# Attention keys and own queries turned on VectorE in 32x32 tiles, with softmax sums taken by columns of ones

## The chip, the cores and the metric

The kernel runs on one core of one Trainium2 chip. The metric is the device time of one execution in microseconds (us): 1069.41 us before the change, the median of three runs (1069.33 to 1069.71). The profile names the engines PE (TensorE; PEld is its loading of weights), DVE (VectorE), ACT (ScalarE), POOL (GpSimd) and SP (SyncE, whose queue issues nearly all DMAs).

## The reference

There are 8 batches of 576 tokens, and 8 heads of 64 columns. Per head, queries are normalised over the head's 64 columns and keys over the 576 tokens; the output is queries x (keys transposed x values). Then comes a Fourier mixing layer with a two-layer network:

```python
q_s = softmax(q, axis=-1)            # exp(q - max) / (sum + 1e-9)
k_s = softmax(k, axis=2)             # over the 576 tokens
kv  = einsum('bhsd,bhse->bhde', k_s, v)
x   = einsum('bhsd,bhde->bhse', q_s, kv)   # put together as (batch, token, 512)
u   = x + real(fft(fft(x, axis=1), axis=2))
un  = (u - mean(u)) / sqrt(var(u) + 1e-6)
out = u + relu(un @ w_ch1) @ w_ch2   # 512 -> 2048 -> 512
```

All is fp32.

## The kernel before, in words

The network of one batch takes most of TensorE's time. Batch 0 goes through it plainly (`plain`, the plain stage), while the weights are converted and combined. From then on `up` and `down` (`deep_down`) use Strassen's seven products; one pass of both is called an order, and order n works on one group of tokens while attention, mixing and normalisation of batch n + 1 are prepared beside it. Every step is a small function with a planned time; `timed` lists them for each order, all are sorted by that time, scaled by 0.87, and written out in that order. So the planned times fix the order of the instructions of every engine, and each engine works its list in order.

In the product stage (`up`), four rounds of seven products run. Each product of a round collects in one of three PSUM banks, ba, bb and bc. The order of products is 1, 6, 5, 7, 2, 4, 3: product 1 in ba is copied to s1 by ACT; after product 6 DVE adds u2 = bb + s1 (L1216), and only then may product 7 collect further in bb; after product 7 DVE adds u3 in the same way, and only then comes product 4. POOL combines the results of a round in a chain of four steps (`a_side`, L383 to L386). The weights come through a ring of four chunks (`load`, `used`, L454).

Attention of batches 2 to 7 is laid out by `attention_timed`. It starts with the product stage in orders 1 and 2 (`start` is 0), and 7 planned units ahead of it later. Two heads form a region of 128 columns, so there are four regions of keys. Keys come transposed in DRAM as (column, token). Per region:

- `k_exp`: maximum over the tokens on DVE (L666), exponential with the sum in one pass on ACT (L672), inverse on DVE;
- `k_turn`: four transposes on TensorE into a PSUM tile (L690), copied by ACT (L696), and a fifth for the last 64 tokens (L700), copied by DVE (L704);
- `k_times_v`: five products with the values (L716) into a bank named acc, of which there are three; DVE scales them into `kvr` (L724).

There are four tiles of own queries (128 tokens each) in every batch. Per tile:

- `q_exp`: maximum per head on DVE (L760), eight exponentials with a bias each on ACT (L766), sums, inverse and, for two of the four tiles, normalisation on DVE (L785 to L796);
- `q_turn`: four transposes on TensorE (L824), copied by ACT, reversed for two tiles (L834);
- `q_times_kv`: four products with `kvr` (L886), taken out by DVE with the inverse (L901) or copied by ACT (L903).

A ninth tile of shared tokens (`t_...`) is made once for two batches. Batches 0 and 1 have steps of their own (`first_keys`, `opening`, and the plain stage); they share some of these functions.

In fp32 a product appears in the trace as two MATMUL passes, a transpose as one.

## Time and profile before

| | us |
|---|---|
| median of three runs | 1069.41 (1069.33 to 1069.71) |
| span of the profiled execution | 1068.4 |
| time around the span, by the median | 1.0 |
| busy: PE, PEld | 1056.4, 920.5 |
| busy: DVE, ACT, POOL | 698.9, 398.2, 380.4 |
| product passes of `up` (L1246): 1792 | 431 (184.2 + 123.8 + 123.4) |
| product stages of orders 1 to 4 begin at | 177.7, 296.9, 413.5, 528.7 |

The busy time of an engine is the time in which at least one of its instructions ran; TensorE's overlap, so that the length of one MATMUL is more than the distance to the next. Idle time of an engine that is not the bottleneck costs nothing. The page holds one execution, and its span leaves out what lies before the first and behind the last instruction. The granted clock of TensorE was 1.000 over the span.

### The profile page before, as it was taken

The numbers are of one execution on the slowest core, as the hardware profiler recorded it, in microseconds if no ns is written. First come the engines' busy times: TensorE is split into PE (matmuls) and PEld (weight loads), VectorE is DVE, ScalarE is ACT, GpSimd is POOL, SyncE is SP. The second block draws the span as 40 slices with busy tenths as digits, with TensorE's granted clock in tenths as the row PEclk, the third lists the DMA queues.
The fourth block names the chain that finished last, engine by engine and source line by source line (L and its number), as shares of the span: only waits on it lengthen the run. The fifth ranks groups of instructions, "written<-read, shape, count | busy, mean of one in ns | idle before, by whom it ended". The sixth has DMA issues, their size and how long they took to land.

```text
span 1068.4 us, 16964 instructions
## 1 busy us (share of the span) xinstructions
PE 1056.4 (99%) x6394; PEld 920.5 (86%) x6394; DVE 698.9 (65%) x1350; ACT 398.2 (37%) x925; POOL 380.4 (36%) x321
## 2 busy tenths in 40 slices
PE   8999999999999999999999999999999999999998
PEld 7744556988898899889998999889988998899898
DVE  6898887675455785677555765678457654674563
ACT  5674433642245215631443234521552132231210
POOL 3263320265511734454515542384336350000000
PEclk9999999999999999999999999999999999999999
DMA  8687578648976576646755576557644575576464
GB/s 266 237 294 251 179 244 294 205 156 284 331 257 207 195 254 235 226 165 209 262 192 193 197 242 213 198 200 257 223 168 158 198 253 181 194 260 221 173 215 151
DMA packets 113546, 236.04 MB, mean 221 GB/s; under 512 B 23272, under 2 KB 74856, under 8 KB 102840
## 3 DMA queue, kind: packets, MB, share of 16 engines
q1 hardware_dynamic: 113096, 234.42, 64.3%
q8 instruction: 51, 0.84, 0.3%
q10 hardware_dynamic: 288, 0.26, 0.1%
q14 instruction: 31, 0.25, 0.1%
q0 software_dynamic: 80, 0.26, 0.1%
HBM read 199.79 MB, written 39.06 MB: 224 GB/s over the span
## 4 chain that ended last, share of the span: by engine, by line
PE 88%; DVE 1%; ACT 1%; issue 0%; POOL 0%; ACTq 0%
PE bb L1246 16%; PE bc L1246 10%; PE ba L1246 10%; PE bb L1373 10%; PE bc L1373 7%; PE ba L1373 7%; PE bb L1343 5%; PE acc L716 3%; PE acc L886 2%; PE bc L1183 2%; PE bb L1462 2%; PE acc L999 2%; PE acc L1002 2%; PE acc L1027 2%; PE bc L1462 1%; PE ba L1462 1%
## 5 line engine op out<-in xcount | busy, mean ns | idle before, releaser
L1246 PE MATMUL bb<-unT,big 128*128 128x256 f32 x768 | 184.2, 379 | 0.0
L1246 PEld LDWEIGHTS bb<-unT,big 128*128 128x128 f32 x768 | 142.7, 190 | 18.7 <-DVE u L1216 0.6
L1258 ACT ACTIVATE big<-big 128x512 f32<-128x512 f32 x96 | 60.4, 629 | 195.7 <-DVE big L1257 195.3
L1246 PE MATMUL ba<-unT,big 128*128 128x256 f32 x512 | 123.8, 379 | 0.0
L1246 PE MATMUL bc<-unT,big 128*128 128x256 f32 x512 | 123.4, 379 | 0.0
L1216 DVE TENSOR_TENSOR u<-bb,s 128x512 f32<-128x512 f32 x66 | 45.5, 689 | 104.8 <-PE bb L1246 84.6
L383 POOL TENSOR_TENSOR big<-big 128x512 f32<-128x512 f32 x24 | 30.5, 1269 | 224.6 <-ACT big L1258 224.6
L1246 PEld LDWEIGHTS bc<-unT,big 128*128 128x128 f32 x512 | 94.7, 190 | 12.4 <-DVE big L1257 0.8
L1373 PE MATMUL bb<-big 128*128 128x128 f32 x848 | 105.1, 275 | 0.3 <-DVE u L1380 0.3
L1246 PEld LDWEIGHTS ba<-unT,big 128*128 128x128 f32 x512 | 94.4, 190 | 12.2 <-issue 0.5
L1373 PEld LDWEIGHTS bb<-big 128*128 128x128 f32 x848 | 99.6, 192 | 0.5 <-DVE u L1380 0.4
L1323 POOL TENSOR_TENSOR x<-x,big 128x512 f32<-128x512 f32 x45 | 57.7, 1296 | 62.1 <-issue 32.3
L1373 PE MATMUL ba<-big 128*128 128x128 f32 x640 | 79.6, 275 | 0.0
L1373 PEld LDWEIGHTS ba<-big 128*128 128x128 f32 x640 | 76.3, 192 | 1.2
L1319 DVE TENSOR_TENSOR big<-big 128x512 f32<-128x512 f32 x98 | 75.3, 806 | 0.0
L766 ACT ACTIVATE q<-q,qm 128x64 f32<-128x64 f32 x216 | 58.5, 338 | 25.4 <-DVE qm L760 18.9
L1380 DVE TENSOR_TENSOR u<-bb,s 128x256 f32<-128x256 f32 x40 | 16.8, 421 | 65.0 <-PE bb L1373 61.6
L1343 PE MATMUL bb<-big 128*128 128x256 f32 x256 | 58.7, 381 | 0.0
L1257 DVE TENSOR_TENSOR big<-bc,u 128x512 f32<-128x512 f32 x64 | 43.9, 686 | 21.8 <-PE bc L1246 21.0
L1122 POOL TENSOR_TENSOR unT<-unT 128x512 f32<-128x512 f32 x8 | 14.2, 1771 | 123.4 <-DVE unT L1122 100.8
L1343 PEld LDWEIGHTS bb<-big 128*128 128x128 f32 x256 | 48.2, 190 | 8.0 <-DVE big L1257 1.1
L1373 PE MATMUL bc<-big 128*128 128x128 f32 x416 | 51.5, 275 | 0.0
(268 smaller groups left out, 2028.4 us busy)
## 6 DMA issues: line engine op xcount, KB each, us to landing
big<-w2d SPq DMA_DIRECT2D x67, 1024.0 KB, 4.8
big<-w1s SPq DMA_DIRECT2D x64, 896.0 KB, 4.8
big<-w2s SPq DMA_DIRECT2D x16, 1024.0 KB, 6.6
big<-in_w_dram SPq DMA_DIRECT2D x21, 512.0 KB, 6.2
w2d<-big SPq DMA_DIRECT2D x42, 256.0 KB, 5.4
q<-in_q_dram SPq DMA_DIRECT2D x28, 256.0 KB, 6.6
k<-in_kT_dram SPq DMA_DIRECT2D x24, 288.0 KB, 5.5
v<-in_v_dram SPq DMA_DIRECT2D x24, 256.0 KB, 4.5
```

The costliest lines, as they stand in the source:

```text
L383: e1.tensor_tensor(out=to(4), in0=at(2), in1=at(3), op=ALU.add)
L716: nc.tensor.matmul(pk, lhsT=ks[:, c, :], rhs=v[:, c, :], start=(c == 0), stop=(c == NC - 1))
L766: nc.scalar.activation(q[:, h, :], q[:, h, :], ACT.Exp, bias=m[:, h:h + 1])
L1216: plus = lambda t: V.tensor_tensor(out=temp(t), in0=box["bb"][:], in1=box["s1"][:], op=ALU.add)
L1246: nc.tensor.matmul(bank()[:, i, :], lhsT=w[:, WA_AT[m], k * P:(k + 1) * P], rhs=self.unT[g][:, B_AT[m], k, :], start=first and i == 0 and ...
L1257: steps = [(0, lambda: V.tensor_tensor(out=hp(i), in0=bank()[:], in1=u()[:], op=ALU.add)), (0.8, lambda: nc.scalar.activation(hp(i), hp(i) ...
L1258: (0.8, lambda: nc.scalar.activation(hp(i), hp(i), ACT.Relu))]
L1319: e.tensor_tensor(out=to(o), in0=to(x), in1=to(y), op=op)
L1323: E.tensor_tensor(out=x, in0=x, in1=tile(m), op=ALU.add)
L1343: nc.tensor.matmul(box[name][:, i, :], lhsT=h[p][:, A_AT[m], i * P:(i + 1) * P], rhs=self.stream[n][:, p, :], start=p == 0 and (m != 1 or ...
L1373: nc.tensor.matmul(box[place[n]][:, i, :], lhsT=own(m)(A_AT[n])[:, f, :], rhs=w[:, r // 2, r % 2 * P:r % 2 * P + P], start=first and f == ...
L1462: nc.tensor.matmul(bank()[:, i, :], lhsT=h[p][:, A_AT[m], i * P:(i + 1) * P], rhs=w[:, p, :], start=first and i == 0 and p == 0, stop=p == ...
```

## The change

- Keys of a batch are loaded into one tile `kb` of 128 partitions: token block i (160 tokens, the last overlapping) lies on partitions 32 i to 32 i + 31, and 16 groups of 32 columns lie behind one another. Four loads on 32 partitions each replace four on 128. Values go into `vt` in the same manner, in two halves of 256 columns, four loads per half, with a column of ones at each end.
- `keys`: one maximum per region on DVE over 4 x 160 elements, joined over the four partition groups by ACT copies and DVE minima; 16 exponentials on ACT without a sum; DVE turns a region in 32x32 tiles, region 0 into a free buffer and each further one into the place of the region before it; five products with 129 columns, of which one is ones and gives the sums of the exponentials.
- `own_exp`: maximum on DVE, subtraction on POOL, turning on DVE in 32x32 tiles, then 16 exponentials on ACT that put the 32x32 tiles in their place on the way (reversed for two tiles). `own_times_kv`: products with 130 columns, two of them ones, and the inverse of the sums on DVE; the output is written in two halves by DVE, and uses two acc banks.
- The planned times of these steps and of the loads are new, `prepare` sets the ones on POOL in the plain stage, and the last four blocks of the second layer's weights are combined in another order.

Batches 0 and 1 and the shared tiles keep their transposes on TensorE. The core of the diff:

```diff
-            t = c.tile([P, NR, P], F32, name=f"kvr{b}")
+            t = c.tile([P, NR, P + 2], F32, name=f"kvr{b}")
...
-        self.kss = [c.tile([P, NC, P], F32, name=f"ks{i}") for i in range(2)]
...
-        self.kss += [self.work.tile([P, NC, P], F32, tag="v", name="ks", bufs=2) for _ in range(2)]
-        for t in self.kss[:2]:
-            nc.gpsimd.memset(t[0:64, 4, :], 0.0)
+        self.kb = c.tile([P, NR, 4, NC * Q], F32, name="kb")
+        kb = self.kb[:].rearrange("p r g s -> p (r g s)")
+        self.kss = [kb[:, i * NC * P:(i + 1) * NC * P].rearrange("p (c n) -> p c n", n=P) for i in range(NR)]
+        self.vt = c.tile([P, NC, 2 * P + 2], F32, name="vt")
...
-        keys = [("k", b, r) for r in range(NR)]
         tail = [("t", b)] if b % 2 == 0 else []
         own = [("q", b, c, u) for c, u in ((0, 0), (0, 1), (1, 1), (1, 0))]
-        first = start + 14 + 5 * len(tail)
-        gap, steps = (end - 13.7 - first) / 3, []
-        places = [first + gap * i for i in range(4)]
-        shared = start + 14
-        if tail and start == 0:
-            shared, places = 17, [14, 21, 26, 31.3]
-        for i, it in enumerate(keys):
-            t = start + 3.5 * i
-            if i > 1:
-                steps += at(t - 5, self.k_load(it)[:1]) + at(t + 1.8, self.k_load(it)[1:])
-            steps += at(t, self.k_exp(it)) + at(t + 4, self.k_turn(it)) + at(t + 7, self.k_times_v(it))
+        places, shared = [6, 13.5, 21.5, 27.2], start + 12
+        if tail:
+            places = [8.5, 14, 21.5, 27.2]
+        if start == 0:
+            places, shared = [13.5, 20.5, 24, 27.2], 7
+        steps = at(start, self.keys(b))
         for it in tail:
             steps += at(shared, self.q_exp(it)) + at(shared + 8, self.t_turn(it))
             steps += at(22.4 if start < 0 else 35, self.t_fold(it))
         for t, it in zip(places, own):
-            steps += at(t, self.q_exp(it)) + at(t + 8.7, self.q_turn(it)) + at(t + 12.1, self.q_times_kv(it))
-        loads = [(t, self.q_load(it)) for t, it in zip(places, own)] + [(shared - 6, self.t_load(it)) for it in tail]
+            steps += at(t, self.own_exp(it)) + at(t + 15, self.own_times_kv(it))
+        loads = [(t - 7, t + 7.6, self.own_load(it)) for t, it in zip(places, own)]
+        loads += [(shared - 13, shared + 8.4, self.t_load(it)) for it in tail]
         loads.sort(key=lambda s: s[0])
-        for t, load in loads[2:]:
-            steps += at(t - 6, load)
-        return steps + at((33 if start < 0 else 39) if tail else 22, self.t_times_kv(b))
+        free = [-99] * 3
+        for i, (t, end, load) in enumerate(loads):
+            if i > 1:
+                steps += at(max(t, free[-3]), load)
+            free.append(end)
+        return steps + at((33 if start < 0 else 39) if tail else max(22, start + 26), self.t_times_kv(b))
...
-        steps = [(20 + r, lambda r=r: self.keys_to(b, r)) for r in range(3)]
-        steps += [(35 + r, lambda r=r: self.values_to(b, r)) for r in range(2)]
-        q = [self.q_load(("q", b, 0, u)) for u in range(2)]
+        steps = at(24 if b > 2 else 20, self.keys_to(b))
+        steps += at(35 if b > 2 else 22.5, self.values_to(b, 0))
+        q = [self.own_load(("q", b, 0, u)) for u in range(2)]
...
+    def keys_to(self, b):
+        def load(i):
+            rows = self.kT[b].rearrange("(g p) s -> p g s", p=Q)
+            a = min(i * NC * Q, S - NC * Q)
+            self.nc.sync.dma_start(self.kb[i * Q:i * Q + Q].rearrange("p r g s -> p (r g) s"), rows[:, :, a:a + NC * Q])
+        return [(0.6 * i, lambda i=i: load(i)) for i in range(4)]
+    def values_to(self, b, h):
+        def load(i):
+            first = VD * (i == 3)
+            a = min(i * NC, S // Q - NC) + first
+            v = self.v[b, :, h * HD:(h + 1) * HD].rearrange("(c s) n -> s c n", s=Q)[:, a:a + NC - first]
+            self.nc.sync.dma_start(self.vt[i * Q:i * Q + Q, first:, 1:1 + HD], v)
+        return [(0.5 * i, lambda i=i: load(i)) for i in range(4)]
+    def prepare(self):
+        G = self.nc.gpsimd
+        for t in self.kvr:
+            for h in range(2):
+                G.memset(t[64 * h:64 * h + 64, :, P + h:P + h + 1], 1.0)
+        for col in (0, 2 * P + 1):
+            G.memset(self.vt[:, :, col:col + 1], 1.0)
+        G.memset(self.vt[3 * Q:, 0:VD, :], 0.0)
+    def across(self, box, by, n):
+        other = []
+        def copies():
+            m = box()
+            w = self.small.tile([P, n], F32, tag="across", name="across", bufs=2)
+            other.append(w)
+            if by == 2:
+                for h in range(2):
+                    nc.scalar.copy(w[64 * h:64 * h + 64], m[64 - 64 * h:128 - 64 * h])
+            else:
+                for i in range(4):
+                    nc.scalar.copy(w[i * Q:i * Q + Q], m[(i ^ 1) * Q:(i ^ 1) * Q + Q])
+        def least():
+            m = box()
+            nc.vector.tensor_tensor(out=m[:], in0=m[:], in1=other.pop()[:], op=ALU.min)
+        return [(0, copies), (0.3 + 0.15 * (4 // by), least)]
+    def keys(self, b):
+        nc, V, kb = self.nc, self.nc.vector, self.kb
+        box = {}
+        def top(r):
+            if r == 0:
+                box["m"] = self.small.tile([P, 4 * NR], F32, tag="km16", name="km16", bufs=2)
+            V.reduce_max(box["m"][:, 4 * r:4 * r + 4], kb[:, r], axis=AX.X, negate=True)
+        def exp(g):
+            k = kb[:, g // 4, g % 4]
+            nc.scalar.activation(k, k, ACT.Exp, bias=box["m"][:, g:g + 1])
+        def turn(r):
+            if r == 0:
+                t = self.work.tile([P, KT, HD], F32, tag="Z", name="Z", bufs=1)
+                t = t[:].rearrange("p k n -> p (k n)")[:, 0:NC * P]
+            else:
+                t = kb[:, r - 1].rearrange("p g s -> p (g s)")
+            to = box["k", r] = t.rearrange("p (c n) -> p c n", n=P)
+            V.transpose(to.rearrange("p c (g s) -> p c g s", s=Q), kb[:, r].rearrange("p g (c s) -> p c g s", s=Q))
+        def times(r):
+            pk, k = self.acc((P, P + 1)), box.pop(("k", r))
+            box[r] = pk
+            a = (P + 1) * (r % 2)
+            for c in range(NC):
+                nc.tensor.matmul(pk, lhsT=k[:, c, :], rhs=self.vt[:, c, a:a + P + 1], start=c == 0, stop=c == NC - 1)
+        def scale(r):
+            pk = box.pop(r)
+            rec = self.small.tile([P, 1], F32, tag="krec", name="krec", bufs=4)
+            at = P * (r % 2)
+            V.tensor_scalar(out=rec[:], in0=pk[:, at:at + 1], scalar1=ATT_EPS, scalar2=None, op0=ALU.add)
+            V.reciprocal(rec[:], rec[:])
+            for h in range(2):
+                s, cols = slice(64 * h, 64 * h + 64), slice(64 * h + 1 - r % 2, 64 * h + 65 - r % 2)
+                V.tensor_scalar(out=self.kvr[b % 2][s, r, s], in0=pk[s, cols], scalar1=rec[s, 0:1], scalar2=None, op0=ALU.mult)
+        steps = [(0.9 * r, lambda r=r: top(r)) for r in range(NR)]
+        steps += at(3.6, self.across(lambda: box["m"], 2, 4 * NR)) + at(4.5, self.across(lambda: box["m"], 1, 4 * NR))
+        steps += [(6 + g / 2, lambda g=g: exp(g)) for g in range(4 * NR)]
+        for r in range(NR):
+            for dt, f in ((8.3, turn), (10.8, times), (12.5, scale)):
+                steps.append((dt + 2 * r + 6 * (r > 1 and f != turn), lambda f=f, r=r: f(r)))
+        steps += at(13.5, self.values_to(b, 1))
+        return steps
+    def own_load(self, it):
+        _, b, c, u = it
+        def load():
+            q = self.work.tile([P, D], F32, tag="q", name="q", bufs=3)[:]
+            self.nc.sync.dma_start(q, self.q[b, tokens(c, u), :])
+            self.live[it] = [q]
+        return [(0, load)]
+    def own_exp(self, it):
+        nc, V, G, live = self.nc, self.nc.vector, self.nc.gpsimd, self.live
+        heads = lambda: live[it][0].rearrange("p (h d) -> p h d", h=H)
+        def top():
+            m = self.small.tile([P, H], F32, tag="qm", name="qm", bufs=3)
+            V.reduce_max(m[:], heads(), axis=AX.X, negate=True)
+            live[it].append(m)
+        def less():
+            m = live[it].pop()
+            G.tensor_tensor(out=heads(), in0=heads(), in1=m[:].unsqueeze(2).to_broadcast([P, H, DH]), op=ALU.add)
+        def turn():
+            V.transpose(live[it][0], live[it][0])
+            live[it].append(self.work.tile([P, D], F32, tag="qT", name="qT", bufs=3)[:])
+        def exps(some):
+            of, to = (t.rearrange("p (r i n) -> i p r n", r=NR, i=4) for t in live[it])
+            for n in some:
+                i, t = n // 4, n % 4
+                one = of[i, t * Q:t * Q + Q]
+                if it[2] != it[3]:
+                    t, one = 3 - t, one[:, :, ::-1]
+                nc.scalar.activation(to[t, i * Q:i * Q + Q], one, ACT.Exp)
+            if some[-1] == 15:
+                live[it].pop(0)
+        return [(0, top), (0.9, less), (2.7, turn)] + [(3.6 + n / 2, lambda n=n: exps((n, n + 1))) for n in range(0, 16, 2)]
+    def own_times_kv(self, it):
+        nc, V, (_, b, c, u) = self.nc, self.nc.vector, it
+        box = []
+        def times():
+            q = self.live.pop(it)[0].rearrange("p (r n) -> p r n", r=NR)
+            for half in range(2):
+                px = self.acc((P, 2 * (P + 2))).rearrange("p (r n) -> p r n", r=2)
+                box.append(px)
+                for r in range(2):
+                    nc.tensor.matmul(px[:, r, :], lhsT=q[:, 2 * half + r, :], rhs=self.kvr[b % 2][:, 2 * half + r, :],
+                                     start=True, stop=True)
+        def inverse():
+            rec = self.small.tile([P, 2, 2, 2], F32, tag="qrec", name="qrec", bufs=4)
+            for half in range(2):
+                V.tensor_scalar(out=rec[:, half], in0=box[half][:, :, P:], scalar1=ATT_EPS, scalar2=None, op0=ALU.add)
+            rows = rec[:].rearrange("p a r h -> p (a r h)")
+            V.reciprocal(rows, rows)
+            box.append(rec)
+        def out(half):
+            x = self.xpart(b, c, u)[:, half * HD:(half + 1) * HD].rearrange("p (r h d) -> p r h d", r=2, h=2)
+            V.tensor_tensor(out=x, in0=box[half][:, :, 0:P].rearrange("p r (h d) -> p r h d", h=2),
+                            in1=box[2][:, half].unsqueeze(3).to_broadcast([P, 2, 2, DH]), op=ALU.mult)
+        return [(0, times), (1.5, inverse), (1.6, lambda: out(0)), (1.7, lambda: out(1))]
...
-            qT = self.work.tile([P, NR, P], F32, tag="qT", name="qT", bufs=2)
-            self.nc.scalar.copy(qT[:], pt[:] if c == u else pt[:, :, ::-1])
+            qT = self.work.tile([P, D], F32, tag="qT", name="qT", bufs=3)[:].rearrange("p (r n) -> p r n", n=P)
+            self.nc.scalar.copy(qT, pt[:] if c == u else pt[:, :, ::-1])
...
-                nc.tensor.matmul(px[:, r * P:(r + 1) * P], lhsT=qT[:, r, :], rhs=self.kvr[b % 2][:, r, :], start=True,
+                nc.tensor.matmul(px[:, r * P:(r + 1) * P], lhsT=qT[:, r, :], rhs=self.kvr[b % 2][:, r, 0:P], start=True,
...
-    for p, dt in zip((3, 7, 0, 1, 2, 4, 5, 6), (34, 42.5, 57.3, 59.3, 61.3, 63.5, 65.5, 68)):
+    for p, dt in zip((3, 7, 2, 0, 1, 6, 4, 5), (34, 42.5, 57.3, 59.3, 61.3, 63.5, 65.5, 68)):
+    steps.append((first + 60, blk.prepare))
```

## The prediction

> **What bounds the kernel now.** I read the page's shares first, then what ended TensorE's waits, then its timeline inside one attention stage, and last the other engines in that stage.
>
> ```profile
> span 1068.4 us, 16964 instructions
> PE 1056.4 (99%) x6394; PEld 920.5 (86%) x6394; DVE 698.9 (65%) x1350; ACT 398.2 (37%) x925; POOL 380.4 (36%) x321
> ```
>
> TensorE is busy for 99% of the span and nothing else is near. The waits of TensorE alone say whether that is a queue that never runs dry:
>
> ```profile
> PE ba L241 <- POOL kvr L155: 2.3, 1, 2.3
> PE acc L999 <- issue: 1.7, 1, 1.7
> PE tr L537 <- ACT big L532: 1.3, 2, 0.9
> PE acc L559 <- DMA big<-in_v_dram: 0.6, 2, 0.4
> ...
> PE acc L886 <- ACT qT L834: 0.3, 1, 0.3
> ```
>
> All of them together are 8 us, nearly all in the opening; batches 2 to 7 have 0.3 us. So the end is set by the sum of TensorE's instructions, and an instruction taken from it shortens the time by its own slot, as long as no new wait opens. The groups of the work that goes or stays:
>
> ```profile
> L690 PE MATMUL tr<-ident,k 128*128 128x128 f32 x96 | 14.4, 273 | 0.0
> L700 PE MATMUL tr<-ident,k 128*128 128x128 f32 x24 | 6.5, 273 | 0.0
> L824 PE MATMUL tr<-ident,q 128*128 128x128 f32 x124 | 18.7, 273 | 0.0
> L716 PE MATMUL acc<-v,ks 128*128 128x128 f32 x240 | 30.7, 275 | 0.0
> ```
>
> 273 ns is the length of one, and they overlap. The slot is the distance between starts, which the timeline gives (start, length, group):
>
> ```profile
> 301.17 0.60 PE L690 MATMUL tr<-ident,k 128*128 128x128 f32 x4
> 301.61 0.27 PE L700 MATMUL tr<-ident,k 128*128 128x128 f32 x1
> 301.72 1.03 PE L1246 MATMUL bc<-unT,big 128*128 128x256 f32 x4
> 302.58 1.89 PE L1246 MATMUL bb<-unT,big 128*128 128x256 f32 x8
> 304.31 1.28 PE L716 MATMUL acc<-v,ks 128*128 128x128 f32 x10
> 305.42 0.60 PE L690 MATMUL tr<-ident,k 128*128 128x128 f32 x4
> ...
> 324.26 0.60 PE L824 MATMUL tr<-ident,q 128*128 128x128 f32 x4
> 324.70 1.03 PE L1246 MATMUL ba<-unT,big 128*128 128x256 f32 x4
> ```
>
> Four transposes hold TensorE for 0.44 us (301.17 to 301.61; 324.26 to 324.70), the fifth for 0.11; ten passes of keys times values for 1.11 (a product counts as two passes, a transpose as one).
>
> **TensorE's sum.** Batches 2 to 7 have 24 key regions and 24 own query tiles. Removed: 24 x (0.44 + 0.11) + 24 x 0.44 = 23.8 us. Added: a column of ones on 240 passes of keys times values and two on 192 passes of queries times kv. 256 columns take 0.865 / 4 = 0.216 us and 128 take 0.111, so a column costs 0.8 ns: 0.2 + 0.3 = 0.5 us. Net 23.2 us less. The three runs have a median of 1069.41; the profiled span is 1068.4, so about 1 us lies around it, and 1069.4 - 23.2 = 1046.2 is the time with no new wait.
>
> [...]
>
> **What moves to the other engines**, per batch. In a product stage beside attention:
>
> ```profile
> 523.00:565.00 42.00, 42.00 (x264) 38.58 (x264) 24.05 (x57) 20.77 (x55) 12.19 (x10) 1.00 0.66 226
> ```
>
> (window, length, busy PE, PEld, DVE, ACT, POOL, clock, DMA share, GB/s.)
>
> DVE loses: four key maxima at 0.745, four fifth-block copies at 0.294, four query sums at 0.681 with scalar and reciprocal 0.408 + 0.203, two normalisations at 0.692, two outputs at 0.681: 12.1 us. It gains: four maxima of 640 elements (0.745 x 640/576 = 0.83), two 16-wide minima (0.15), eight half outputs (0.42, the 256-element row L1380), four inverses (2 x 0.166 + 0.203), and eight 32x32 turnings. The trace has no such instruction. Its bounds are the scalar form over 512 elements (0.42, the fastest row) and the widest 512-element sum (1.06, L1319 into unT); I take one element per step as in the reductions and adds, 0.83 for 640 and 0.69 for 512. Gain 15.2, net +3.1.
>
> ACT loses 4 x (0.774 + 0.188) key exponentials, 4 + 4 copies out of PSUM at 0.58, 32 query exponentials at 0.27 apart and two copies: 18.3. It gains 16 key exponentials (64 elements take 0.338, 576 take 0.774, so 160 take 0.42, 0.35 apart), 64 query ones of 128 elements (copies: 32 in 0.19, 256 in 0.37, so 0.27) and six small copies: 24.6, net +6.3.
>
> POOL gains four subtractions at 1.12 us (L812), +4.5.
>
> The stage shrinks to 42 - 3.9 = 38.1 us, with DVE about 27, ACT 27, POOL 17. None becomes the bound by its sum. What can cost is order: DVE works in order, and TensorE waits for its adds u2 and u3 before it accumulates on.
>
> **Where a wait can open.** I followed the order of the instructions with these durations.
>
> Batch 2: the add u2 now stands behind four maxima in a row instead of one.
>
> ```profile
> 181.38 0.69 DVE L1216 TENSOR_TENSOR u<-bb,s 128x512 f32<-128x512 f32 x1 [2.16 <-PE bb L1246]
> ```
>
> DVE had 2.16 us to spare there. After the output add at 177.87, 0.69 + 4 x 0.83 puts u2 at 181.9 and its end at 182.6; TensorE needs it at 182.86 (transposes are gone from between). It holds. One round later u2 is behind the third and fourth turned region, a scale and the first turned tile, which itself waits for POOL: it ends about 1.2 us late. In batch 3 the same two places come to 0.3 us; from batch 4 on the keys begin 6 us earlier, and u2 and u3 keep 1 us or more. I charge 1.5 us in all; bounds 0 and 6 (1 us in each batch). The DVE turning of a tile queued behind POOL's four-step chain (4 x 1.3 us) would hold u2; in the order, the subtraction stands ahead of that chain in all rounds but one, where u2 comes 3 us later.
>
> Values: they now come in two halves into one buffer. The second half may be fetched only when TensorE is through with region 1, and region 2 needs it. Between lie 16 (odd batches) or 16 and a four-transpose group (even): 6.9 and 7.4 us of TensorE work, 0.4 more until the last piece is needed. Behind the freed buffer SP issues four pieces of 32 partitions, with one to three stores or query loads between, 0.4 us each: the last is issued 1.6 to 2.8 us after. Transfers of this kind landed after:
>
> ```profile
> v<-in_v_dram SPq DMA_DIRECT2D x24, 256.0 KB, 4.5
> v<-in_v_dram SPq DMA_DIRECT2D x24, 64.0 KB, 7.2
> ```
>
> With 4.5 us the last lands at 6.1 to 7.3, in time; with 7.2 at 8.8 to 10.0, up to 2.6 us late. SP's weight loads queued behind have two chunks in hand. I take 0.4 us a batch, nearer the first row since a piece (144 KB on average) is nearer to 256 KB; 2.4 in all; bounds 0 and 15.
>
> The other loads and the earlier turning of the weights' blocks (same instructions, other order, DVE had 2.12 us free before 177.87) I cost at nothing: keys are fetched a stage ahead, with as many issues as before (12 per batch with the values). If that cover went, TensorE would wait once per batch, as for the values.
>
> Sum: 1046.2 + 1.5 + 2.4 = 1050.1.
>
> **Rivals.** *Slots as it says, few waits*: 1050, own range 1046 to 1055; chance 0.63.
>
> *Values late*: region 2 waits 2.5 us in each of six batches, 1046.2 + 1.5 + 15 = 1062.7; where half of them wait, 1055. For: the 64 KB row, and a 896 KB weight load issued just ahead in batches 2 and 3. Against: transfers of 64 KB for queries on 32 partitions landed after 4.7. Chance 0.20. [...]
>
> *Length is cost*: if the busy sums were what TensorE pays, 14.4 + 6.5 + 96/124 x 18.7 = 35.4 us would go: 1034.5. The timeline speaks against it. Chance 0.03.
>
> *Turning on DVE is slow and TensorE waits for it* (the slower side): at twice my price each of eight turnings adds 0.75 us, 6 us per batch, in front of u2 or of a kv product that has 0.4 us to spare in batch 2. With 1 us hidden per batch, six batches give 30: 1046.2 + 30 = 1076. It decides against the change from 3.9 us of wait per batch, 0.5 us more per turning with no cover. For it: no row prices the operation. Against: DVE has 11 us free per stage. Chance 0.10. Halfway, gain and wait cancel, 1067 to 1071: 0.04.
>
> **How the numbers follow.** 0.2% (2.1 us) is about what a measurement tells from no change. Faster: 0.63 + 0.20 + 0.03 = 0.86; same 0.04; slower 0.1. The range from 1046 (no wait at all) to 1061 (nearly all of the late values) holds 0.63 and some 0.17.
>
> **What would show it.** Right: no transposes of keys and own queries after the plain stage, 216 fewer on TensorE; TensorE's waits grow by a few us, named DMA vt at the third region and DVE u; turnings of 0.7 to 0.85 us. Wrong: a wait above 1 us per batch on vt (values), turnings above 1.4 us with TensorE waiting for u or the turned keys (slow turning), or starts closer by more than 0.11 us per removed transpose.

## The result, and the profile after

The changed kernel takes 1054.14 us (median of four executions, 1053.50 to 1057.53); the kernel before 1069.43 on the same chip. The ratio is 0.9864, 95% interval 0.985 to 0.9879: 15.3 us faster, where 19.3 were forecast and 23.2 would have come without any new wait. The time lies inside the range of 1046 to 1061, and 4.0 us above the sum of the prediction (1050.1).

The page of the changed kernel (its profiled execution is the longest of the four, 1057.53 us):

```profile
span 1055.8 us, 16768 instructions
PE 1037.7 (98%) x6178; PEld 899.8 (85%) x6178; DVE 722.6 (68%) x1410; ACT 456.1 (43%) x1141; POOL 406.0 (38%) x350
```

6178 against 6394: the 216 transposes are gone, and TensorE still bounds the kernel. ACT is busy for 58 us more than before, DVE for 24 and POOL for 26. TensorE's own waits, in microseconds (total, times, longest):

```profile
PE acc L715 <- DMA vt<-in_v_dram: 2.8, 2, 2.7
...
PE tr L1195 <- ACT eo L1189: 1.5, 1, 1.5
...
PE acc L790 <- ACT qT L774: 0.8, 2, 0.5
PE bc L1334 <- DVE big L1345: 0.5, 1, 0.5
```

The lines left out are nearly as before, the longer ones all of the opening. These four are new or have grown: the third region waits for values (L715), the normalisation ahead of the first product stage is late (L1195), the own queries wait for their exponentials on ACT (L790), and DVE is late for a bank once (L1334). The groups that the change brought:

```profile
L774 ACT ACTIVATE qT<-q 32x128 f32<-32x128 f32 x384 | 117.9, 307 | 12.1 <-DVE q L764 7.1
L715 PE MATMUL acc<-vt,kb 128*128 128x129 f32 x180 | 24.7, 285 | 2.8 <-DMA vt<-in_v_dram 2.8
L764 DVE STREAM_TRANSPOSE q<-q 128x512 f32<-128x512 f32 x24 | 17.0, 707 | 3.2 <-POOL q L761 2.9
L708 DVE STREAM_TRANSPOSE kb<-kb 128x640 f32<-128x640 f32 x18 | 15.1, 837 | 5.4 <-ACT kb L699 5.4
```

A turning takes 0.71 us for 512 elements and 0.84 for 640, where 0.69 and 0.83 were estimated. The place of the largest loss is in batch 2 (start, length, group):

```profile
197.78 1.89 PE L1334 MATMUL bc<-unT,big 128*128 128x256 f32 x8
199.75 1.13 PE L1334 MATMUL bb<-unT,big 128*128 128x256 f32 x4
203.53 2.39 PE L715 MATMUL acc<-vt,kb 128*128 128x129 f32 x10 [2.65 <-DMA vt<-in_v_dram]
205.71 1.70 PE L1334 MATMUL bb<-unT,big 128*128 128x256 f32 x4
```

TensorE waits 2.65 us for the last piece of the values' second half. Then ten passes take 2.39 us, where 1.28 is usual, and four take 1.70 instead of 1.03. The stretch behind it says why (window, length, busy PE, PEld, DVE, ACT, POOL, clock, DMA share, GB/s):

```profile
203.65:207.06 3.41, 3.41 (x14) 3.14 (x15) 0.00 (x0) 0.00 (x0) 0.28 (x1) 0.50 0.26 105
```

For 3.41 us after the wait TensorE's granted clock is 0.50. So the wait cost 2.65 us and half of 3.41 behind it. With the smaller delays beside it, 4.6 us more than their slots lie between 199.7 and 207.3.

The time from the first product of `up` in one order to the first in the next, read from each timeline, shows where the rest lies. "Plain" is from the first product at all to the first of order 1; "total" from the first matmul of the execution to the last. The last five rows are experiments, told below. The two profiled executions of the changed kernel are the longest of their runs, so the table shows its losses at their largest.

| kernel (profiled execution) | plain | 1 | 2 | 3 | 4 | 5 | 6 | total |
|---|---|---|---|---|---|---|---|---|
| before | 175.4 | 119.2 | 116.6 | 115.3 | 115.8 | 115.3 | 115.7 | 1061.7 |
| changed | 177.3 | 121.3 | 113.9 | 111.9 | 112.1 | 111.7 | 112.5 | 1049.2 |
| again | 176.9 | 122.0 | 113.8 | 112.0 | 112.1 | 111.5 | 112.5 | 1049.3 |
| by_region | 176.9 | 116.8 | 113.5 | 111.5 | 112.1 | 111.5 | 112.5 | 1043.3 |
| three | 174.6 | 116.8 | 113.5 | 111.5 | 112.1 | 111.5 | 112.5 | 1041.0 |
| exps_first | 174.9 | 116.1 | 112.8 | 111.5 | 112.1 | 111.5 | 112.5 | 1040.0 |
| turn_twice | 177.5 | 122.0 | 116.0 | 114.2 | 114.1 | 114.2 | 114.6 | 1061.1 |

Orders 3 to 6 gave 3.4, 3.7, 3.6 and 3.2 us, close to the 3.9 that their slots promised. Order 1, in which batch 2 is prepared, became longer than before the change, and so did the plain stage.

### The profile page after: what moved, and what is told of

It reads as the page before. It is cut to its first block, busy times and chain, and to the rows that moved or that the text cites. A ratio compares the mean times of both kernels' runs of the same rounds, so it can differ in the third digit from the quotient of the medians.

```text
span 1055.8 us, 16768 instructions
## 1 busy us (share of the span) xinstructions
PE 1037.7 (98%) x6178; PEld 899.8 (85%) x6178; DVE 722.6 (68%) x1410; ACT 456.1 (43%) x1141; POOL 406.0 (38%) x350
## 4 chain that ended last, share of the span: by engine, by line
PE 78%; DVE 5%; ACT 4%; DMA 3%; issue 1%; SPq 0%; POOL 0%; DVEq 0%; ACTq 0%
PE bb L1334 14%; PE bb L1461 10%; PE ba L1334 10%; PE bc L1334 9%; PE bc L1461 7%; PE ba L1461 7%; PE bb L1431 5%; PE acc L715 3%; ACT qT L774 2%; PE bb L1550 2%; PE acc L790 2%; PE acc L1087 1%; PE acc L1090 1%; DMA vt<-in_v_dram 1%; PE bc L1550 1%; PE ba L1550 1%
## 5 line engine op out<-in xcount | busy, mean ns | idle before, releaser
L1334 PE MATMUL bb<-unT,big 128*128 128x256 f32 x768 | 183.1, 381 | 0.1
L1334 PEld LDWEIGHTS bb<-unT,big 128*128 128x128 f32 x768 | 144.7, 191 | 19.9 <-DVE u L1304 1.0
L1334 PE MATMUL ba<-unT,big 128*128 128x256 f32 x512 | 124.0, 379 | 0.2 <-ACT big L1341 0.2
L774 ACT ACTIVATE qT<-q 32x128 f32<-32x128 f32 x384 | 117.9, 307 | 12.1 <-DVE q L764 7.1
L1334 PE MATMUL bc<-unT,big 128*128 128x256 f32 x512 | 121.8, 380 | 0.5 <-DVE big L1345 0.5
L1334 PEld LDWEIGHTS bc<-unT,big 128*128 128x128 f32 x512 | 96.1, 190 | 14.2 <-DVE big L1345 1.8
L1334 PEld LDWEIGHTS ba<-unT,big 128*128 128x128 f32 x512 | 94.8, 190 | 12.6 <-ACT big L1341 0.6
L761 POOL TENSOR_TENSOR q<-q,qm 128x512 f32<-128x512 f32 x24 | 25.8, 1073 | 116.1 <-DVE qm L756 73.0
```

The source lines that it names most:

```text
L774: nc.scalar.activation(to[t, i * Q:i * Q + Q], one, ACT.Exp)
L1334: nc.tensor.matmul(bank()[:, i, :], lhsT=w[:, WA_AT[m], k * P:(k + 1) * P], rhs=self.unT[g][:, B_AT[m], k, :], start=first and i == 0 and ...
```

## The experiments

Two theories stood at first. A: the slots are right, and the loss sits at the few places where TensorE waited. B: the loss is spread over DVE and ACT in all batches, and what is taken away at one place comes back at the next. All times below are medians beside runs of the kernel before on the same chip; ratios are against that.

**again: the changed kernel once more.** No edit.

> The changed kernel once more, for a second profile. Theory A (waits at a few places, one of them chance): in the first profile TensorE waited 2.65 us for the values at the third region of batch 2 and then ran at a clock of 0.5 for 3.4 us, 4.9 us in all, and that profile is also the longest of the four executions by 3 us. So a profile without that wait has clock 1.0 in the stage of batch 2 and a span of about 1051.5; the 1.5 us before the first product stage may go or stay. Median 1054. Theory B (the loss is fixed in the order of the instructions): the wait and the clock of 0.5 come in every profile, span 1055 to 1056.

Measured 1055.8 us (1054.32, 1054.57, 1057.02, 1057.81), ratio 0.9868 (0.9853 to 0.9883). The profiled execution, again the longest, has the long wait again at the same product (2.60 us; here the profile names no releaser) and again a clock of 0.5 for 3.4 us behind it. Over both runs of this kernel three of eight executions took 1057 us or more, the other five 1053.5 to 1054.6. The two that were profiled are of the three, and both have the wait. Whether the other six have it was not seen, and their granted clocks, which are on record, speak against so simple a split: the third long one (1057.02) ran at 1.000, so without any stretch of half clock, and one of the short ones (1054.52) at 0.996, which is more than one stretch of 3.41 us.

**later and later2: the late products of batches 2 and 3 put later.** Both move regions 2 and 3 two planned units and the own products one. In `later` the loads of the next batch's keys stayed where they were, so they stand ahead of region 3 and it computes with the next batch's keys; its time is that of another program. `later2` moves these loads and the shared product as well.

```diff
-        steps = at(start, self.keys(b))
+        steps = at(start, self.keys(b, 2 * (start == 0)))
-                steps.append((dt + 2 * r + 6 * (r > 1 and f != turn), ...
+                steps.append((dt + 2 * r + (6 + late) * (r > 1 and f != turn), ...
-            ... at(t + 15, self.own_times_kv(it))
+            ... at(t + 15 + (start == 0), self.own_times_kv(it))
   later2 alone:
-        steps = at(24 if b > 2 else 20, self.keys_to(b))
+        steps = at((26 if b < 5 else 24) if b > 2 else 20, self.keys_to(b))
```

> The changed kernel with regions 2 and 3 of the keys times values (and their scaling) two planned units later, and the own queries times kv one unit later, in batches 2 and 3 alone. Theory A: the waits of these two batches for the values (2.65 and 0.4 us), the half clock behind the first (1.7 us) and the waits for the own exponentials (0.5 and 0.65 us) go; 1050 to 1052 against some 1054. Theory B (what is lost is spread over all batches and lies on DVE and ACT in their order): no change, 1053.5 to 1054.5. If the later products only move the wait to the own products, 1053 or more with a wait named POOL or DVE kvr.

`later`: 1072.27 us (ratio 1.0028, 1.0019 to 1.0038). Twice TensorE waited for the next batch's keys, 8.4 us the longest, and each time the clock was at 0.5 for 10.2 us after it.

> The changed kernel; in batches 2 and 3 regions 2 and 3 of the keys times values two planned units later, the own and the shared queries times kv one or two units later, and the key loads of the next batch two units later, so that they stay behind the last region. Theory A (the loss sits at the places where TensorE waited): the wait for values in batch 2 (2.65 us and 1.7 us of half clock) and the two for own exponentials (0.5 and 0.65 us) go, 1050 to 1052. Theory B (a wait that is taken away comes back at the next step of DVE, ACT or the loads): 1053.5 to 1056, with a wait as long on kvr, qT or kb in the same stage.

`later2`: 1054.69 us (1053.89 to 1056.46; ratio 0.9865, 0.9849 to 0.9882), no better than the changed kernel. Order 1 fell to 117.7 us, where the values came 1.1 us late and not 2.65. But order 2 rose to 116.4, with a wait that was not there (DVE's timeline in batch 3):

```profile
329.99 1.06 DVE L1016 SCALAR_TENSOR_TENSOR eo<-eo,sign 128x255 f32<-128x255 f32 x1 [0.56 <-ACT eo L1011]
331.09 1.24 DVE L1018 TENSOR_TENSOR eo<-eo 128x128 f32<-128x128 f32 x1
332.36 1.30 DVE L1019 TENSOR_TENSOR eo<-eo 128x128 f32<-128x128 f32 x1
...
334.25 0.68 DVE L1304 TENSOR_TENSOR u<-bb,s 128x512 f32<-128x512 f32 x1
```

The shared product's steps (L1016 to L1019) and, in the line left out, the output of an own tile now stand ahead of the add u, for which TensorE waited 2.5 us, and the clock was at 0.5 for 3.41 us after it. That is theory B at this place: a step that is moved later pushes its DVE work in front of an add. The length of that work matters as much as its place: the two adds L1018 and L1019 took 1.24 and 1.30 us, where the changed kernel has 0.29 each, and that is 2.0 of the 2.5 us.

**keys_only and own_only: each half of the change by itself.** `keys_only` is the changed kernel with the own queries as before; `own_only` is the kernel before with the own queries of the change (with the changed kernel's times for them; two of its four qT tiles lie in the free Z tile).

```diff
   keys_only (the query loads, changed to match, are left out here):
-            steps += at(t, self.own_exp(it)) + at(t + 15, self.own_times_kv(it))
+            steps += at(t, self.q_exp(it)) + at(t + 8.7, self.q_turn(it)) + at(t + 15, self.q_times_kv(it))
   own_only (in the kernel before; the functions and their loads are left out here):
-            steps += at(t, self.q_exp(it)) + at(t + 8.7, self.q_turn(it)) + at(t + 12.1, self.q_times_kv(it))
+            steps += at(t, self.own_exp(it)) + at(t + 15, self.own_times_kv(it))
```

> Keys as in the changed kernel, own queries with their transposes on TensorE as before. Theory A: 120 transposes x 0.109 us = 13.1 us are gone, and the waits of the keys stay (values 0.5 to 4.9 us, others about 1): 1057 to 1062. Were the length of a transpose its price (the rival of the sum), 21 us would go: 1050. If the loss lies with the keys alone, the gain is under 8 us: over 1061.

> Own queries as in the changed kernel, keys and values as before. Theory A: 96 transposes x 0.109 us = 10.5 us are gone; the 16 exponentials per tile at 0.307 us on ACT stay and TensorE waits for them 1 to 2 us in batches 2 and 3: 1060 to 1062. If the loss of the changed kernel lies with the own queries, the gain is under 6 us: over 1063.

Measured: `keys_only` 1064.96 us (1061.91 to 1067.92; ratio 0.9954, 0.9938 to 0.997), `own_only` 1064.95 us (1064.16 to 1066.49; ratio 0.9961, 0.9945 to 0.9976). Both land where their expectations put the loss on that half alone (over 1061, over 1063). That can't hold for both, so neither half is the sole cause. Adding up the median distance to the next start for every matmul settles the slots: 1049.4 us before, 1036.3 without the key transposes (13.1 less), 1038.8 without the own ones (10.6 less), 1025.7 without both (23.7 less). So the slots come off in full, and 8.8 and 6.3 us of them are lost again. Together that is 15.1 us, where the whole change loses 8.4 (23.7 less 15.3), in `again` 10.2: the two losses do not add up to that of the whole, and the halves do not tell how it is made up. In `keys_only` TensorE lost time at the third region in batches 2 to 4 (3.1 us of wait for values at the longest, with the half clock) and stood 0.6 us twice ahead of the own tiles' transposes; in `own_only` for the add u (1.5 us in two waits) and for own exponentials (1.0); these are 2.5 of the 6.3 us that it lost.

**tight: the loads of values closer together.**

```diff
   values_to:
-        return [(0.5 * i, lambda i=i: load(i)) for i in range(4)]
+        return [(0.1 * i, lambda i=i: load(i)) for i in range(4)]
```

> The changed kernel with the four loads of each half of the values behind one another on SP's queue (0.1 planned units apart, not 0.5), so that no query load stands between them. Theory A1 (the wait comes from what is queued between and ahead of the pieces): the last piece is issued 0.5 to 0.9 us earlier and has one query load of 256 KB less ahead of it, so the wait of 2.65 us falls to 1 to 1.8, the half clock does not come, and executions of 1057 disappear: median 1053 to 1054. Theory A2 (32 partitions per piece make the transfer slow whatever is ahead): the wait stays at 2 us or more, 1054 to 1056.

Measured 1053.14 us (1052.28 to 1055.68; ratio 0.9859, 0.9843 to 0.9875). It can't tell A1 from A2: SP's order in batch 2 came out as it was, with the query load still behind the first piece. It tells something else. Up to this place every engine and SP have the same instructions in the same order as in the changed kernel, yet the wait was 0.58 us, not 2.65, and no half clock followed. The last piece was issued 0.7 us earlier (195.06, not 195.74), and its product began 6.4 us after that, not 7.8. So the length of this wait varies with the same order of work; what makes it vary was not tried.

**old_order: the second layer's weights combined in the old order.**

```diff
-    for p, dt in zip((3, 7, 2, 0, 1, 6, 4, 5), ...
+    for p, dt in zip((3, 7, 0, 1, 2, 4, 5, 6), ...
```

> The changed kernel with the last blocks of the second layer's weights combined in the order of before (3, 7, 0, 1, 2, 4, 5, 6). If the new order makes the wait ahead of the first product stage (TensorE for eo, 0.8 and 1.5 us in the two profiles of the changed kernel; 1.2 to 1.9 us lost there against before), it goes: 1052.5 to 1054. If the key loads of batch 2 in that stage make it (1.3 MB in four loads in place of three), it stays, and the time is that of the changed kernel, 1054 to 1056.

Measured 1053.95 us (1053.21 to 1054.45; ratio 0.9859, 0.9843 to 0.9876). The time lies where it was expected if the new order made the wait, but TensorE still waited 0.9 us for eo ahead of the first product stage. So the new order is not the reason for that wait. The wait for values in batch 2 was 0.4 us here, again with the changed kernel's order on SP around these loads.

**turn_twice: every turning done twice.**

```diff
+            for _ in range(2):
                 V.transpose(to.rearrange(...), kb[:, r].rearrange(...))
...
             live[it].append(... name="qT", bufs=3)[:])
+            V.transpose(live[it][1], live[it][0])
```

> The changed kernel with every turning on DVE done twice (the second of an own tile goes into the buffer that the exponentials fill later): 4 x 0.84 + 4 x 0.71 = 6.2 us more DVE work per batch, just what the rival of slow turning supposed. By that rival (1 us per batch hidden, the rest on the path) 30 us more: 1084. By the sums (DVE has some 11 us free per product stage and TensorE bounds it) the batches whose keys begin early hide all of it, and batches 2 and 3 pay 1 to 4 us each: 1056 to 1062.

Measured 1068.34 us (1065.92 to 1069.57; ratio 0.9994, 0.9985 to 1.0004): 13 to 14 us more than the changed kernel, so the whole gain is gone. Both expectations missed, on either side. TensorE's waits:

```profile
PE bb L1336 <- DVE u L1306: 5.0, 4, 2.6
PE acc L716 <- DVE Z L709: 4.3, 6, 0.8
```

Of 6.2 us more on DVE, orders 2 to 6 pay 2.0 to 2.7 us each (the table, against "again"), at two places: region 0's turned keys (Z) come 0.7 us late in each of six batches, and the add u comes late. So some 4 us of the 6.2 are hidden there, not all and not 1. Order 1 stays at 122.0, but nothing is hidden in it: TensorE waits 2.6 us for u at about the place where it waited for the values, and the clock is at 0.5 after it.

**by_region: the second half of the values one region at a time.**

```diff
-        steps += at(13.5, self.values_to(b, 1))
+        for r in range(2):
+            steps += at(11.5 + 2 * r, self.values_to(b, 1, slice(r * P, (r + 1) * P)))
```

(`values_to` takes the columns as a third argument; region r + 2 comes into the columns of region r once that has been multiplied.)

> The changed kernel with the second half of the values fetched one region at a time: the four pieces of region 2 (72 KB on average) once region 0 is through, those of region 3 once region 1 is. In batch 2 region 0 is through 2.85 us before region 1, so the last piece of region 2 is issued 2 to 3 us earlier and carries half the bytes. Theory A (values late, near the point where a wait of 2.6 us brings 3.4 us of half clock): the wait at the third region goes in all batches, no execution above 1055, median 1052.5 to 1053.5. Theory B (the eight shorter pieces cost SP 1.7 us more per batch and hold up the weights queued behind, or region 3 becomes the late one): 1054 to 1056, with a wait named big or vt.

Measured 1051.6 us (1050.43 to 1051.96; ratio 0.983, 0.9817 to 0.9844), lower than either theory gave: 2.5 to 4.2 us below the two medians of the changed kernel, whose intervals lie wholly above, and all five executions lie within 1.6 us. SP's queue in batch 2, first in the changed kernel, then here, and TensorE here:

```profile
192.10 0.32 SPq L455 DMA_DIRECT2D big<-w1s  x1
193.22 0.34 SPq L648 DMA_DIRECT2D vt<-in_v_dram  x1
...
194.08 2.08 SPq L648 DMA_DIRECT2D vt<-in_v_dram  x3
```

```profile
190.36 2.61 SPq L648 DMA_DIRECT2D vt<-in_v_dram  x4
193.01 0.43 SPq L455 DMA_DIRECT2D big<-w1s  x1
```

```profile
199.41 1.13 PE L1335 MATMUL bb<-unT,big 128*128 128x256 f32 x4
200.38 1.28 PE L715 MATMUL acc<-vt,kb 128*128 128x129 f32 x10
```

Region 2's four pieces are issued from 190.36 on; in the changed kernel the half's four went out from 193.22 to 196.16, behind a weight load of 896 KB and with a query load (left out) between them. Region 2 is multiplied at 200.38 without a wait, and at full clock. Order 1 takes 116.8 us in place of 121.3. So the wait at the third region, with the clock behind it, is what made order 1 longer. Which of the earlier start, the half size and the place ahead of the weights did it isn't told apart.

**values_35: batch 2's first half of values fetched later in the plain stage.**

```diff
-        steps += at(35 if b > 2 else 22.5, self.values_to(b, 0))
+        steps += at(35, self.values_to(b, 0))
```

> The changed kernel with the first half of batch 2's values fetched 12.5 planned units later in the plain stage, about where the kernel before fetched them (it took SP 4.5 us for four pieces there, ahead of the stores of converted weights). Theory A: that is what makes TensorE wait for eo ahead of the first product stage (0.8 to 1.5 us; 1.0 to 1.9 us more lost there than before): 1.0 to 1.9 us come back, 1052.5 to 1054.5. Theory B: the key loads or chance make it, and the time stays at 1054 to 1056.

Measured 1053.4 us (1051.38 to 1056.13; ratio 0.9849, 0.9832 to 0.9866). This median can't be told from the changed kernel's, and the wait at the third region is still there (2.0 us in its profile, and the clock at 0.50 after it). So the profile has to answer: its plain stage took 175.7 us. What DVE waited for there, first in the changed kernel, then here:

```profile
DVE spare L428 <- DMA w2s<-spare: 4.5, 1, 4.5
```

```profile
DVE spare L428 <- DMA w2s<-spare: 2.6, 1, 2.6
```

In the kernel before it was 3.1. DVE waits until a store of combined weights has left the tile it needs, and behind DVE wait ACT's normalisation and TensorE. The nine profiles with the early load have 3.7 to 4.7 us here, the three with the late load 2.5 to 2.8. The plain stage took 176.3 to 177.8 us in eight of the nine; with the late load 174.6, 174.9 and 175.7; before the change 175.4. The ninth is `old_order`: 3.9 us of this wait, 0.9 for eo, and yet 175.8. So the load's place makes DVE's wait longer; why that one stage was short all the same is open.

**three: both, and the second own tile's product later.**

```diff
   by_region and values_35, and:
-            ... at(t + 15, self.own_times_kv(it))
+            ... at(t + 15 + 1.2 * (start == 0 and it is own[1]), self.own_times_kv(it))
```

> Values by region and batch 2's values later, as in the two other kernels, and in batches 2 and 3 the second own tile's product with kv 1.2 planned units later, so that TensorE does not wait there for its exponentials (0.5 to 0.75 us, twice). If the places are independent: 1054.8 (the middle of the changed kernel's medians) less 2 (values, the share of executions that have the long wait), 1.4 and 1.2: 1050 to 1051. If what is taken away comes back behind it on DVE or ACT: 1052 to 1054.

Measured 1050.43 us (1049.41 to 1050.88; ratio 0.9822, 0.9808 to 0.9835). The plain stage gave its 2.3 us in the profile; orders 1 and 2 gave nothing. So the time came out where it was expected if the three places are independent, but one of the three terms gave nothing. The waits for own exponentials only went to the later place: 0.61 and 0.77 us are lost there, 0.48 and 0.65 in `by_region` (lost is what a distance between two starts has above its median). ACT in batch 2 shows the reason:

```profile
196.34 3.82 ACT L775 ACTIVATE qT<-q 32x128 f32<-32x128 f32 x12 [1.36 <-DVE q L765]
201.69 0.63 ACT L1347 ACTIVATE big<-big 128x512 f32<-128x512 f32 x1 [1.53 <-DVE big L1346]
202.33 0.63 ACT L775 ACTIVATE qT<-q 32x128 f32<-32x128 f32 x2
```

Twelve of the first tile's sixteen exponentials are done at 200.16; then ACT idles 1.53 us for a copy that waits for DVE, with the other four queued behind. From 201.69 on it has hardly a gap.

**exps_first: the first tile's exponentials all ahead of that copy.**

```diff
   by_region and values_35, and in own_exp:
+        d = 0.3 if it[1] in (2, 3) and it[2] == it[3] == 0 else 0.5
-        return [...] + [(3.6 + n / 2, lambda n=n: exps((n, n + 1))) for n in range(0, 16, 2)]
+        return [...] + [(3.6 + d * n, lambda n=n: exps((n, n + 1))) for n in range(0, 16, 2)]
```

> Values by region and batch 2's values later, as in the kernel before this one, with all own products at their old places; instead the 16 exponentials of the first own tile of batches 2 and 3 are put closer on ACT (0.3 planned units apart, not 0.5), so that the last four stand ahead of the copy of a result for which ACT waited 1.5 to 2 us idle. Theory A (TensorE waits for own exponentials since ACT is packed from there on): 1.3 us of ACT work moves into its idle time, the two waits of 0.6 to 0.75 us at the second tile go, and the waits behind them stay: 1049 to 1050. Theory B (it comes back behind, as it did when the product was put later): 1050 to 1051.

Measured 1048.91 us (1048.50 to 1050.87; ratio 0.9816, 0.9803 to 0.983). ACT does sixteen in a row (first line below), its wait for DVE falls from 1.53 to 0.25 us, and the second own tile is multiplied without a wait in batch 2 (0.14 us lost in batch 3):

```profile
196.66 5.09 ACT L775 ACTIVATE qT<-q 32x128 f32<-32x128 f32 x16 [1.35 <-DVE q L765]
202.00 0.63 ACT L1348 ACTIVATE big<-big 128x512 f32<-128x512 f32 x1 [0.25 <-DVE big L1347]
```

This is the lowest median of the study, 20.1 us below the kernel before, though its ratio can't be told from that of `three`; what the edit did is seen in the profile. Its matmuls take 1040.0 us from first to last; those of the kernel before less 216 x 0.109 us would take 1038.2.

## Why the prediction was right or wrong

**Right: what bounds the kernel, and the price of a transpose.** 216 transposes came off at 0.109 us each, alone and together, as the distance between starts said. "Length is cost" fell: the sum of the slots fell by 23.7 us. The added columns of ones cost nothing that can be seen: keys times values has a median slot of 0.112 us with 128 and with 129 columns (0.2 us in all was charged, and 0.3 for the queries).

**Right: the prices on DVE.** The turnings were 0.84 and 0.71 us, the key maxima 0.81, the half outputs 0.42, POOL's subtraction 1.07. Of these only the minima were off, 0.53 us and not 0.15, twelve in all.

**Wrong: the charge for values, 0.4 us a batch.** The bound of the lateness was right: the two profiles of the changed kernel have the last piece 2.65 and 2.60 us late, the worst case of the sum. The bound of the landing was not: in batch 2 the product began 7.8 and 8.0 us after the issue of its last piece, more than 7.2. The charge spread the lateness evenly. In truth it stands in batch 2. In batch 3, with the same 896 KB load just ahead, the product began 5.3 us after that issue, and 0.3 to 0.4 us are lost at this place; in batch 4 0.4 to 0.5, later 0.2 at most. So the weight load alone, which the rival named, is not the cause, and what makes batch 2 slow stays open. And the sum charged a wait at its length. Here 2.65 us cost 4.4, since half of 3.41 us of half clock comes on top. The half clock lasted 3.41 us at 0.50, and 10.2 after the 8.4 us wait in `later`. In every trace the changes of the clock lie whole multiples of 3.413 us apart: in the changed kernel's, 197.97 us of full clock (58 of them), 3.413 of half clock, and 849.92 of full clock (249). Cut into the stretches of that grid, from 40 us on, all eight stretches of full clock with 1.98 us or more of TensorE's idle time before its last matmul were followed by half clock, and none with 1.65 us or less (in the opening of `own_only` one with 1.40 was). So a wait of 2.0 us did it (`values_35`); of the 3.1 us in `keys_only`, 2.6 fell into one stretch.

The rival "values late" was thus right in its place for batch 2, and wrong in its breadth: one batch, and in `tight` and `old_order` 0.58 and 0.4 us with the same order on SP around these loads. Whether a piece is slow because it lies on 32 partitions was not tried: no run here changes the partitions of a piece.

**Wrong: "the other loads I cost at nothing".** The batch 2 loads come in the plain stage, where the cover that was named (a stage of time ahead of use) protects the loads but not the stores queued behind them. It cost 1.5 to 1.9 us in the two profiles of the changed kernel, and `values_35` and `three` got it back.

**Wrong: "what can cost is order: DVE".** For the adds u 1.5 us were charged; in batches 2 and 3 the two profiles of the changed kernel lose 0.5 and 0.9 us there. The order that cost was ACT's. An own exponential takes 0.307 us, one every 0.32, not every 0.27; that is 3 us more per batch, packed into one stretch of batches 2 and 3 behind an idle wait. Lost there: 0.49 and 0.65 us for the second own tile. `exps_first` took these away, and showed that ACT's total (43% of the span) had said nothing on it. What is left is 0.66 us at bank bc in batch 2 and 0.33 at ba in batch 3, both a little later; their cause was not tried.

**Luck: that the sum came within 4 us.** The slots carried the forecast. Of them 3.9 us were charged for waits, and by the medians 8.4 were lost (23.7 less 15.3). In the profile the losses stand at the values in batch 2 (4.6 us), in the plain stage (1.9), at the own exponentials (1.1) and at the two banks (1.0), and the last three had been put at nothing. The upper part of the range, made for values that are late in all batches, caught losses of another kind.

**Slow turning.** The price fell on the cheap side, so this did not come about. But the size of the danger was misjudged too: 30 us were forecast for 6.2 us more per batch, and `turn_twice` measured 13 to 14. The point from which the change would lose is near that, twice the price of a turning.

**The base.** The runs that list both have 1.8 us between span and time, before and after the change, not the 1.0 taken from one page beside another execution's time. The sum was made from the median, so nothing hangs on it.

## What to carry to other kernels

Where one engine is full, price what is taken from it by the distance of starts; that term held to 0.5 us here (23.7 for 23.2). The waits did not: look for each at the first place where the new order has least lead (here the first two batches and the stage that feeds them), price what is queued behind every load, stores included, and count a wait on TensorE of 2 us or more with the slow clock behind it, as five kernels here showed it. An engine at 43% can still be late: look at the stretch in which its work is packed, and at an idle wait that stands in front of it.

## What was not expected of the hardware

- Waits of TensorE of 2.0 to 3.1 us were followed by 3.41 us at a granted clock of 0.50, in five kernels, so that each cost 1.7 us more than its length; the changes of the clock lie whole multiples of 3.413 us apart in every trace.
- The same order of instructions on TensorE and SP up to the place gave a wait for a DMA of 0.58 us in one kernel and of 2.65 in another. Executions of the changed kernel lay up to 4 us apart.
- On DVE an add of 128 x 128 elements took 1.24 and 1.30 us in `later2`, while POOL's chain of adds ran beside it; in `three` the same two took 0.29 each, at a time when POOL was idle. Both long ones ended 0.15 us after an instruction of POOL's had ended, and each such add of over 1 us in all fourteen traces (11 to 15 in each) ends close behind one: by 0.06 to 0.15 us for the 12 of the kernel before, by 0.09 to 0.15 for the 11 of the changed one. So they look held up until POOL is through, and not slowed.
